# Two placements on TensorE in a fused RWKV-7 and SoLU kernel: transposes inside the solve/scores stretch of two slots, and the mean of w_out

## The chip, the core and the metric

The kernel runs on one core of one Trainium2 chip. The metric is the device time of one execution, in microseconds. Before the change it is 621.36 us, the median of 3 runs (620.54 to 622.96).

## The reference

Two blocks follow each other. The first is a linear recurrence over 768 time steps for 4 batches x 8 heads, with a state of 40 x 40 per head. The second is a feed-forward layer with 1024 hidden units over the 3072 resulting rows of 320.

```python
for t in range(S):                                   # S = 768
    y[:, :, t] = einsum('bhd,bhde->bhe', r_t, state)
    Sa = einsum('bhde,bhe->bhd', state, a_t)
    state = state * w_t[:, :, None, :] - Sa (x) b_t + v_t (x) k_t
x = y as (3072, 320)
h = x @ w_in                                         # 320 x 1024
solu = h * exp(h - max h) / (sum exp(h - max h) + 1e-9)
ln = (solu - mean(solu)) / sqrt(var(solu) + 1e-6) * g_ln
out = ln @ w_out                                     # 1024 x 320
```

## The kernel before

**Slots.** Time is cut into chunks of 64 steps, 12 per sequence, and the batches are taken in two pairs, so there are 24 pieces of work (chunk and pair), each with 128 rows: 2 batches x 64 steps. One main loop runs over slots `i` from -1 to 27. It is a software pipeline: slot `i` prepares piece `i+5` (decay, transposes, the chunk's coupling matrix `nt`), brings the inverse for piece `i+1`, does the recurrence proper of piece `i`, and does the feed-forward layer of pieces `i-2` to `i-4`. All engines run a schedule written out by hand: each engine's instructions stand in the order in which the loop body calls them, and an engine never goes past an instruction that waits. "Slot 5" below is the iteration with `i = 5`.

**The order within a slot, on TensorE.** By the names of the tiles: `pu` (the solve, `solved`, 64 passes of small products: every float32 product runs as two passes), `ps` (the scores of piece i+1, `scores`, 64 passes), `pst` (four transposes of the state, `stated`), `pa` (four transposes of the input `a` of piece i+5, `front`), a product of `h` (`hidden`), `pb` (`front_b`), `pei` (`decay_turned`), another product of `h`, `pcum` (`decay`), four products of `po` (`output`), `py` (`couple`), `pnt` (`norm`), `pl` (`answered`), the other four of `po`, `pz` (`close`), then `pyo`, `px` (`read`, `carried`, `driven`), `plnT` (`folded`), and between further products of `h` the transposes `pk`, `pv` and `pr` of the next piece (`attend_kv`, `attend_r`). Slots 0 to 3 have no feed-forward products or only some of them.

**Buffers that tie the engines together.** PSUM has three pools: `banks` (two buffers, used in turn by `pu`, `ps`, `py`, `pnt`, `pl`, `pz`, `pyo`, `px`), `bank` (two buffers, in turn for the transposes, `pcum`, `pmean` and `po`) and one buffer `h`. So `pz` takes the buffer of `pnt`, and can start when VectorE has read `pnt` (the mask that writes `nt`, L375); `pei` takes the buffer of `pa` and waits for VectorE's `aT` (L366); `pl` takes that of `py` and waits for ScalarE's `wy` (L469).

**VectorE and ScalarE.** VectorE does the masks (`psi`, `lv`, `nt`, `lu`, all L375), `aT`, the softmax part (`nmax`, `e`, statistics), the reading of `pyo` (`x` L619, `tot` L634), a block inverse in small steps (`prod` L428, `uu` L430) spread over the slots, `flip` (`tu`, L457), and the conversion of the weights. ScalarE copies transposes out of PSUM, takes exponentials and logarithms (`lw`, `ei`, `inv`), and does part of the conversion. GpSimd scales `kb` (L337) with `inv` and issues DMAs.

**The weights and their mean.** `w_in` and `w_out` arrive as 64-bit words and are converted to float32 piece by piece in slots -1 to 3 (`split`, called by `narrow`: `scale` on VectorE and ScalarE L182 to L191, then three VectorE operations L193 to L195). `w_out`, already times `g_ln`, stands in `w2` in 8 chunks of 128 rows. Its mean over the 1024 rows is summed on TensorE: the constant matrix `mean` (2^-10 everywhere) times each chunk, summed in PSUM and copied out by ScalarE (L231). It is done in three parts; a later part first brings the sum so far back with a product by the identity (L227). `centred` then subtracts the mean from `w2` in slot 4 (L236). The three calls before the change are

```python
if i == 1 + LAG:                      # slot 2, between answered (pl) and close (pz)
    mean = mean_of(0, 4)
if i == 2 + LAG:                      # slot 3, at the same place
    mean = mean_of(4, 6, mean)
...
if i == 2 + LAG:                      # slot 3, at its very end
    mean = mean_of(6, NF, mean)
```

Of the kernel before, what the change touches and what calls it, by code (L numbers as in the profile page):

```python
# [9 lines left out]
FP32 = mybir.dt.float32  # L10
# [7 lines left out]
P = 128  # L18
# [4 lines left out]
AHEAD = 5  # L23
LANDS_NEXT = {2: 6, 3: 7, 5: 8, 6: 9, 7: 10, 8: 11, 10: 12}
LAG = 1
LN_EXP = "natural_log_exp_and_others"


# [20 lines left out]
def kernel(  # L49
# [18 lines left out]
    nc = tc.nc  # L68
    B, H, S, D = r.shape
    DM = H * D  # L70
    DFF = moe_w_in.shape[1]
# [13 lines left out]
    ps2 = ctx.enter_context(tc.tile_pool(name="ps2", bufs=1, space=PSUM))  # L85
# [3 lines left out]

    nc.scalar.preload_act_table_set(LN_EXP)  # L90

# [4 lines left out]
    def c_(name):  # L96
        lo, hi = where[name]
        return cst[:, lo:hi]

    ident, tri = c_("ident"), c_("tri")  # L100
# [31 lines left out]
    w2 = const.tile([P, NF, DM], FP32, name="w2")  # L132
# [6 lines left out]
    def bank(name):  # L139
        return ps3.tile([P, 512], FP32, tag="bank", name=name)  # L140
# [56 lines left out]
    begun = []  # L197
# [23 lines left out]
            nc.scalar.mul(out=x, in_=pg[:, 0:NF], mul=2.0 ** y)  # L221


    def mean_of(lo, hi, begun=None):
        t = bank("pmean")
        if begun is not None:
            nc.tensor.matmul(t[:, 0:DM], lhsT=ident, rhs=begun, start=True, stop=False)  # L227
        for c in range(lo, hi):
            nc.tensor.matmul(t[:, 0:DM], lhsT=c_("mean"), rhs=w2[:, c, :], start=begun is None and c == lo, stop=c == hi - 1)
        mean = two.tile([P, DM], FP32, tag="osb", name="mean", bufs=1)  # L230
        nc.scalar.copy(out=mean, in_=t[:, 0:DM])  # L231
        return mean
# [35 lines left out]
    def heads(ap):  # L268
        return ap.rearrange("p (h d) -> p h d", d=D)
# [13 lines left out]
    def ok(i):  # L283
        return 0 <= i < N
# [29 lines left out]
    def logged(i):  # L314
        lw = st[i]["lw"] = two.tile([P, DM], FP32, tag="lw", name="lw", bufs=1)
        nc.scalar.activation(out=lw, in_=st[i]["raw_w"].rearrange("p h d -> p (h d)"), func=AF.Ln)

    def decay(i):
        if not ok(i):
            return  # L320
        d = st[i]
        if "lw" not in d:
            logged(i)
        t = (bank("pcum") if i > 5 else ps2.tile([P, DFF], FP32, tag="h", name="h"))[:, 0:DM]
        nc.tensor.matmul(t, lhsT=c_("cum"), rhs=d["lw"], start=True, stop=True)
        nc.scalar.activation(out=ei_t[0][:, :, 0:D], in_=heads(t), func=AF.Exp)
        inv = d["inv"] = two.tile([P, DM], FP32, tag="inv", name="inv", bufs=4)
        nc.scalar.activation(out=inv, in_=t, func=AF.Exp, scale=-1.0)
# [17 lines left out]
    def tokens(name, bufs=1):  # L346
        return two.tile([P, 2, 4, C], FP32, tag=name, name=name, bufs=bufs)
# [6 lines left out]
    def decay_turned(i):  # L354
        if not ok(i):
            return
        ex = st[i]["ex"] = ex_t[i % (AHEAD + 2)]
        nc.scalar.copy(out=ex[0:W2, :, :, 1:], in_=turned("ei", ei_t[0]))

    def front(i):  # L360
        if not ok(i):
            return
        d = st[i]
        t = turned("a", d["raw_a"])
        aT = d["aT"] = tokens("aT", AHEAD)
        nc.vector.tensor_tensor(out=aT[0:W2], in0=t, in1=d["ex"][0:W2, :, :, 0:C], op=ALU.mult)  # L366
# [92 lines left out]
    def couple(i):  # L459
        if not ok(i):  # L460
            return
        d = st[i]
        t = banks("py")
        for u in in_turn(lambda p, q, g, h: (p ^ h, p)):
            p, q, g, h = u
            j = 2 * q + g
            x = half(p ^ h)
            mm(t[half(p), h, j * Q:j * Q + Q], d["nt"][x, h, j], d["tu"][x, 4 * h + j, 0:Q])
        nc.scalar.activation(out=wy[:, :, :, 0:Q], in_=t[:, :, 0:4 * Q].rearrange("p h (j c) -> p h j c", j=4),  # L469
                             func=AF.Copy, scale=c_("neg_hi"))  # L470
# [26 lines left out]
    def stated(i):  # L497
        if not ok(i):
            return
        d = st[i]  # L500
        bp, ci = where_(i)
        if ci:
            t = bank("pst")
            for x in range(4):
                nc.tensor.transpose(out=t[0:W2, x * P:(x + 1) * P],  # L505
                                    in_=st_t[bp][:, 2 * x:2 * x + 2].rearrange("p a b -> p (a b)")[:, 0:W2], identity=ident)
            d["s"] = two.tile([P, 4, P], FP32, tag="s", name="s", bufs=1)
            nc.scalar.copy(out=d["s"][0:W2], in_=t[0:W2].rearrange("p (x t) -> p x t", x=4))
# [47 lines left out]
    def solved(i):  # L556
        if not ok(i):
            return
        d = st[i]
        t = banks("pu")  # L560
        for u in in_turn(lambda p, q, g, h: (p ^ h, q)):
            p, q, g, h = u
            at, x = (2 * h + g) * C, half(p ^ h)
            mm(t[half(q), p ^ h ^ q, at:at + C], x0[x, h, 2 * q + g], d["tu"][x, 4 * h + 2 * q + g, Q:])
        for u in in_turn(lambda p, q, g, h: (p ^ h, p)):
            p, q, g, h = u
            at, x = 256 + (2 * q + g) * D, half(p ^ h)
            mm(t[half(p), h, at:at + D], d["tu"][x, 4 * h + 2 * q + g, Q:], x0[x, h, 2 * q + g, 0:D])
        nuT = d["nuT"] = tokens("nuT")
        lu = d["lu"] = two.tile([P, H, W2], FP32, tag="lu", name="lu", bufs=1)  # L570
        nc.scalar.mul(out=nuT[0:W2], in_=t[0:W2, :, 0:256].rearrange("p b (j c) -> p b j c", j=4), mul=-1.0)
        nc.scalar.mul(out=lu.rearrange("p (j h) c -> p h j c", h=2)[:, :, :, C:],
                      in_=t[:, :, 256:256 + 4 * D].rearrange("p h (j d) -> p h j d", j=4), mul=-1.0)
# [67 lines left out]
    def left(i):  # L641

        if not ok(i):
            return
        x, xT = st[i]["x"], st[i]["xT"]
        for h in range(2):
            at = C * h
            nc.gpsimd.dma_start(out=xT[3 * D:P, h], in_=x[at:at + P - 3 * D, 2])
            for to in (Q * h, C + Q * h):
                nc.gpsimd.dma_start(out=xT[to:to + Q, 2], in_=x[at + P - 3 * D:at + D, 2])  # L650
# [82 lines left out]
    def some(n, kept=0):  # L733
        while len(steps) > kept and n:
            if next(steps[0], steps) is steps:
                steps.pop(0)
            else:
                n -= 1
# [75 lines left out]
    narrowed = {-1: (0, 1, 0), 0: (0, 1, 1), 1: (1, 0, 2), 2: (0, 1, 2), 3: (1, 0, 1)}  # L814
    for i in range(-1, N + 3 + LAG):
        j, m = i + AHEAD, i - LAG
        pieces = shares.get(i, (0, 5, 4, 4) if i % GRP else (3, 5, 4, 5))
        some_weights = narrowed.get(i, (0, 0, 0))
        if i >= 1:
            bring(i + 1)  # L820
        if i >= 0:
            load_values(i + 2)
        narrow(0, pieces[0])

        solved(i)
        if i >= 0:
            scores(i + 1)
        if i >= 0:
            load_keys(j + 3, "w")
        load_keys(j + 2, "bak")  # L830

        stated(i)
        front(j)
        hidden(m - 2, ((0, 1),))
        if i == 3 + LAG:
            centred(mean)
        narrow(some_weights[1], pieces[1])
        front_b(j)
        if ok(j + 2):
            logged(j + 2)  # L840
        decay_turned(j + 1)
        hidden(m - 2, ((1, 1),))
        flip(i + 1)
        highest(m - 2)
        scaled(j + 1)
        left(i - 1)
        decay(j + 2)
        output(m - 3, 0)

        some(pieces[2])  # L850
        couple(i + 1)
        exped(m - 2)
        norm(j)
        answered(i)
        weighed(m - 2)
        spreadof(m - 2)
        if ok(j) and j % GRP == GRP - 1:
            begin_inverse(j // GRP)
        if i == 0:
            turn_g()  # L860
        if i == 1 + LAG:
            mean = mean_of(0, 4)
        if i == 2 + LAG:
            mean = mean_of(4, 6, mean)
        output(m - 3, 1)

        close(i + 1)
        read(i, True)
        carried(i + 1)
        narrow(some_weights[2], pieces[3], ok(j) and j % GRP == GRP - 1)  # L870
        by_value(i + 2)
        if ok(m - 1):
            hidden(m - 1, ((2, 0), (2, 1)))
        fence()
        read(i, False)
        driven(i + 1)
        leave(i)
        begin_narrow(narrowed.get(i + 1, (0,))[0])
        folded(m - 2)
        hidden(m - 1, ((0, 0),))  # L880
        attend_kv(i + 2)
        hidden(m - 1, ((1, 0),))
        attend_r(i + 2)
        if i == 2 + LAG:
            mean = mean_of(6, NF, mean)
# [30 lines left out]
```

## Time and profile before

| what | value |
|---|---|
| median of 3 runs | 621.36 us (620.54 to 622.96) |
| the profiled execution | 617.47 us, its span 615.7 us |
| mean granted clock of TensorE | 0.938 of full speed |
| TensorE busy | 547.3 us (89%) |
| VectorE busy | 448.7 us (73%) |
| ScalarE busy | 265.6 us (43%) |
| GpSimd busy | 257.7 us (42%) |
| start of pu in slots 1, 2, 3, 4 | 89.59, 108.71, 136.46, 160.38 us |
| start of pu in slots 5, 6, 15, 16 | 182.09, 204.72, 399.23, 421.68 us |

All durations used below come from this one profiled execution. In the profile, "PE" is TensorE's product stream, "PEld" its weight loads, DVE is VectorE, ACT is ScalarE, POOL is GpSimd and SP the engine that only issues DMAs. L257 is the line of a helper that issues most products, so those are told apart by the tile they write. A row of a timeline merges neighbouring instructions of one kind: start, time from the first one's start to the last one's end (pipelined passes overlap), what it is, how many, and in brackets how long the engine stood still before it and what ended that. "issue" there means that nothing that the profile shows was awaited.

### The profile page before, as it was taken

What the parts mean: (1) busy time and instruction counts of PE and PEld (TensorE: products, weight loads), DVE (VectorE), ACT (ScalarE), POOL (GpSimd) and SP (SyncE); (2) the same over time, 40 slices, a digit from 0 to 9 for tenths busy, and PEclk for the clock granted to TensorE, in tenths of its full rate; (3) what the DMA queues carried; (4) which work ended last, traced back from release to release, by engine and by line L of the source; (5) the groups of instructions that cost most, each with busy time, mean ns of one, the idle gap of its engine ahead of it and who ended that gap; (6) DMA issues with size and microseconds to landing.
All of it is one profiled execution on the core that took longest, in us unless ns stands there. A gap on an engine that the chain in (4) does not pass through costs nothing.

```text
span 615.7 us, 26656 instructions
## 1 busy us (share of the span) xinstructions
PE 547.3 (89%) x11453; PEld 397.4 (65%) x11453; DVE 448.7 (73%) x1262; ACT 265.6 (43%) x548; POOL 257.7 (42%) x424
## 2 busy tenths in 40 slices
PE   4555587689899999999999999999999999999994
PEld 3334476566576777777777677777777676676652
DVE  4797978979968869868868868688698688443431
ACT  4434455454443544454454445444433343342221
POOL 3462272472452472473365355534624631322200
PEclk9666767789999999999999999999999999999998
DMA  8986895664445454564565574564532612310100
GB/s 166 156 157 132 176 176 107 139 137 84 82 105 98 94 118 94 97 118 99 94 122 97 95 127 97 111 110 82 109 56 53 122 44 44 65 35 26 28 19 21
DMA packets 213901, 59.93 MB, mean 97 GB/s; under 512 B 199120, under 2 KB 208952, under 8 KB 213784
## 3 DMA queue, kind: packets, MB, share of 16 engines
q1 hardware_dynamic: 195512, 33.78, 32.5%
q0 software_dynamic: 11568, 19.78, 13.9%
q10 hardware_dynamic: 6704, 4.67, 2.7%
q8 instruction: 90, 1.47, 1.0%
q14 instruction: 27, 0.22, 0.1%
HBM read 40.10 MB, written 13.37 MB: 87 GB/s over the span
## 4 chain that ended last, share of the span: by engine, by line
PE 71%; DVE 15%; DMA 4%; issue 3%; ACT 3%; SPq 1%; POOL 1%; ACTq 0%; DVEq 0%; POOLq 0%
PE po L723 16%; PE h L257 15%; PE pyo L257 7%; DVE prod L428 4%; DVE uu L430 4%; PE pu L257 4%; PE plnT L712 4%; PE ps L257 3%; PE px L257 3%; PE py L257 2%; PE pl L257 2%; PE pz L257 2%; PE pst L505 2%; PE pr L342 1%; PE pei L342 1%
## 5 line engine op out<-in xcount | busy, mean ns | idle before, releaser
L257 PE MATMUL h<-w_in,xT 128*128 128x512 f32 (+1 forms) x288 | 123.0, 610 | 0.0
L723 PE MATMUL po<-w,lnT 128*128 128x320 f32 x384 | 112.7, 438 | 0.5 <-ACT lnT L713 0.5
L430 DVE TENSOR_TENSOR uu<-uu,prod 128x30 f32<-128x30 f32 (+4 forms) x360 | 102.1, 284 | 12.4
L428 DVE TENSOR_TENSOR prod<-blk,uu 128x30 f32<-128x30 f32 (+4 forms) x360 | 97.6, 271 | 9.6
L723 PEld LDWEIGHTS po<-w,lnT 128*128 128x128 f32 x384 | 71.0, 190 | 32.6 <-issue 4.1
L401 POOL DMA_DIRECT2D nt_dram<-nt x20 | 18.9, 943 | 120.0 <-DVE nt L375 98.5
L375 DVE TENSOR_TENSOR psi<-ps,cst 128x512 f32<-128x512 f32 x24 | 16.6, 690 | 66.6 <-PE ps L257 66.6
L701 POOL TENSOR_TENSOR rs<-c,mhalf 128x1 f32<-128x1 f32 x24 | 13.5, 561 | 112.1 <-DVE c L700 103.2
L650 POOL DMA_DIRECT2D xT<-x x96 | 48.7, 512 | 0.0
L257 PEld LDWEIGHTS h<-w_in,xT 128*128 128x128 f32 (+1 forms) x288 | 37.4, 189 | 9.2 <-issue 8.1
L670 DVE TENSOR_REDUCE nmax<-h 128x1 f32<-128x1024 f32 x24 | 28.6, 1193 | 18.6 <-PE h L257 18.6
L412 POOL DMA_DIRECT2D blk<-nt_dram x46 | 36.6, 802 | 10.8 <-issue 6.8
L257 PE MATMUL pyo<-lv,kb 64*64 64x104 f32 x768 | 37.8, 266 | 2.2
L257 PEld LDWEIGHTS pyo<-lv,kb 64*64 64x64 f32 x768 | 23.9, 140 | 20.9 <-issue 20.8
L638 POOL TENSOR_TENSOR st<-tot,ex 104x160 f32<-104x160 f32 x44 | 21.8, 512 | 36.6 <-DVE tot L634 23.5
L257 PE MATMUL pyo<-lu,kb 64*64 64x104 f32 x768 | 36.7, 258 | 0.0
L469 ACT ACTIVATE wy<-py,cst 128x256 f32<-128x256 f32 x24 | 11.4, 473 | 56.2 <-PE py L257 56.2
L280 POOL DMA_DIRECT2D raw_r<-in_r_dram x48 | 33.9, 709 | 0.0
L727 ACT ACTIVATE osb<-po,rs 128x320 f32<-128x320 f32 x24 | 12.7, 527 | 48.5 <-PE po L723 32.9
L554 ACT COPY x<-px 128x320 f32<-128x320 f32 x24 | 10.2, 425 | 54.1 <-PE px L257 54.0
L678 ACT ACTIVATE e<-h,nmax 128x1024 f32<-128x1024 f32 x24 | 26.6, 1108 | 14.3 <-DVE nmax L670 14.3
L684 DVE TENSOR_TENSOR e<-h,e 128x1024 f32<-128x1024 f32 x24 | 29.2, 1217 | 4.6 <-ACT e L678 4.6
(128 smaller groups left out, 1162.6 us busy)
## 6 DMA issues: line engine op xcount, KB each, us to landing
blk<-nt_dram POOLq DMA_DIRECT2D x46, 128.0 KB, 4.4
nt_dram<-nt POOLq DMA_DIRECT2D x20, 256.0 KB, 3.5
raw_w<-in_w_dram SPq DMA_DIRECT2D x48, 80.0 KB
a<-in_a_dram SPq DMA_DIRECT2D x48, 80.0 KB
raw_r<-in_r_dram POOLq DMA_DIRECT2D x48, 80.0 KB, 3.1
lv<-in_v_dram SPq DMA_DIRECT2D x48, 80.0 KB
out_dram<-osb ACTq DMA_DIRECT2D x24, 160.0 KB
raw_b<-in_b_dram SPq DMA_DIRECT2D x44, 80.0 KB
```

The lines of the kernel that those rows point to most:

```text
L257: nc.tensor.matmul(o, lhsT=lhsT, rhs=rhs, start=start, stop=stop, skip_group_check=True)
L280: queue.dma_start(out=x[half(p), :, 0:D], in_=ap[2 * bp + p, :, ci * C:(ci + 1) * C, :].rearrange("h t d -> t h d"))
L412: queue.dma_start(out=nb[home:home + Q], in_=blocks[n][:, Q * e:Q * e + Q, Q * e:Q * e + Q])
L428: nc.vector.tensor_tensor(out=t, in0=nb[:, j:j + 1, j + 1:Q].to_broadcast([P, n_c, m]), in1=u[:, 0:n_c, j:j + 1].to_broadcast([P, n_c, m]) ...
L430: nc.vector.tensor_tensor(out=u[:, 0:n_c, j + 1:Q], in0=u[:, 0:n_c, j + 1:Q], in1=t, op=ALU.subtract)
L638: nc.gpsimd.tensor_tensor(out=to3(old), in0=to3(tot[0:W2]), in1=ex[:, :, 2 * q:2 * q + 2, C:].to_broadcast([W2, 2, 2, D]), op=ALU.mult)
L650: nc.gpsimd.dma_start(out=xT[to:to + Q, 2], in_=x[at + P - 3 * D:at + D, 2])
L670: nc.vector.tensor_reduce(out=nmax, in_=d["h"], axis=AX.X, op=ALU.max, negate=True)
L678: nc.scalar.activation(out=e, in_=d["h"], func=AF.Exp, bias=d["nmax"], accum_out=d["esum"])
L684: nc.vector.tensor_tensor(out=d["e"], in0=d["h"], in1=d["e"], op=ALU.mult)
L712: nc.tensor.transpose(out=t[:, j * P:(j + 1) * P], in_=d["e"][:, f * P:(f + 1) * P], identity=ident)
L723: nc.tensor.matmul(d["out"][:, 0:DM], lhsT=d["lnT"][:, f, :], rhs=w2[:, f, :], start=f == 0, stop=f == NF - 1)
```

## The change

In slots 5 and 15 the calls `stated(i)` and `front(j)`, which transpose the state of piece `i` and the input `a` of piece `i+5`, stand between `solved(i)` and `scores(i+1)` instead of after `scores(i+1)` and the loads of later pieces. On TensorE `pst` and `pa` then come before `ps`; on VectorE `aT` comes before `psi` and `lv`; on ScalarE and in the DMA queues the order stays.

The mean's first part shrinks from four chunks to three and is summed in the buffer `h`, not in a `bank`: two products stand in slot 2 between `pb` and `pei`, the third between `pei` and `pcum`, and its copy on ScalarE between `ex` and `ei`. The second part grows from two chunks to three and moves in slot 3 from behind `pl` to before `py`; its copy moves ahead of `wy` and of the exponential of `h`. The third part stays. The number of products is the same.

```diff
+THIN = (5, 15)
...
+    def mean_part(t, lo, hi, start, stop=True):
+        for c in range(lo, hi):
+            nc.tensor.matmul(t[:, 0:DM], lhsT=c_("mean"), rhs=w2[:, c, :], start=start and c == lo, stop=stop and c == hi - 1)
...
+    def mean_kept(t):
         mean = two.tile([P, DM], FP32, tag="osb", name="mean", bufs=1)
         nc.scalar.copy(out=mean, in_=t[:, 0:DM])
         return mean
...
         solved(i)
+        if i in THIN:
+            stated(i)
+            front(j)
         if i >= 0:
             scores(i + 1)
         if i >= 0:
             load_keys(j + 3, "w")
         load_keys(j + 2, "bak")
 
-        stated(i)
-        front(j)
+        if i not in THIN:
+            stated(i)
+            front(j)
         hidden(m - 2, ((0, 1),))
...
         front_b(j)
         if ok(j + 2):
             logged(j + 2)
+        if i == 1 + LAG:
+            first = ps2.tile([P, DFF], FP32, tag="h", name="mean")
+            mean_part(first, 0, 2, True, False)
         decay_turned(j + 1)
         hidden(m - 2, ((1, 1),))
         flip(i + 1)
         highest(m - 2)
         scaled(j + 1)
         left(i - 1)
+        if i == 1 + LAG:
+            mean_part(first, 2, 3, False)
+            mean = mean_kept(first)
         decay(j + 2)
         output(m - 3, 0)
 
         some(pieces[2])
+        if i == 2 + LAG:
+            mean = mean_of(3, 6, mean)
         couple(i + 1)
...
-        if i == 1 + LAG:
-            mean = mean_of(0, 4)
-        if i == 2 + LAG:
-            mean = mean_of(4, 6, mean)
         output(m - 3, 1)
```

More of the change, by code (lines that the diff above doesn't have):

```diff
@@ L221, in turn_g, with mean_of @@
             nc.scalar.mul(out=x, in_=pg[:, 0:NF], mul=2.0 ** y)
-    def mean_of(lo, hi, begun=None):
+    def mean_part(t, lo, hi, start, stop=True):
+        for c in range(lo, hi):
+            nc.tensor.matmul(t[:, 0:DM], lhsT=c_("mean"), rhs=w2[:, c, :], start=start and c == lo, stop=stop and c == hi - 1)
+    def mean_of(lo, hi, begun):
         t = bank("pmean")
[L226 to L229, printed above, removed]
+        nc.tensor.matmul(t[:, 0:DM], lhsT=ident, rhs=begun, start=True, stop=False)
+        mean_part(t, lo, hi, False)
+        return mean_kept(t)
+    def mean_kept(t):
         mean = two.tile([P, DM], FP32, tag="osb", name="mean", bufs=1)
```

## The prediction

> **What bounds the kernel now.** I read the page first: TensorE is busy for 89% of the span, and the chain that ended last is TensorE for 71% of it. The 40 slices show two regimes. Up to slice 9 (about 135 us) the clock digit jumps between 6 and 9 and VectorE is as full as TensorE; from there on TensorE is full at 9.
>
> ```profile
> PE 547.3 (89%) x11453; PEld 397.4 (65%) x11453; DVE 448.7 (73%) x1262; ACT 265.6 (43%) x548; POOL 257.7 (42%) x424
> PE   4555587689899999999999999999999999999994
> DVE  4797978979968869868868868688698688443431
> PEclk9666767789999999999999999999999999999998
> ```
>
> Both edits must therefore be read in their own stretch. For slots 5 and 15 I listed TensorE's timeline around each slot's pu (slot 5 starts at 182.09 us, slot 15 at 399.23 us; column 1 is the start, column 2 the time from first start to last end). Of all slots from 4 to 18 these two alone have a wait on TensorE:
>
> ```profile
> 182.09 0.69 PE L257 MATMUL pu<-tu,x 64*64 64x64 f32 x32
> 183.54 0.57 PE L257 MATMUL ps<-rT,vT 40*64 40x64 f32 x25
> 184.94 0.34 PE L257 MATMUL ps<-rT,vT 40*64 40x64 f32 x7 [0.83 <-issue]
> 185.21 0.64 PE L505 MATMUL pst<-cst,st 128*104 128x128 f32 x4
> ...
> 401.91 0.34 PE L257 MATMUL ps<-rT,vT 40*64 40x64 f32 x7 [0.66 <-issue]
> ```
>
> No tile is awaited ("issue"), and both stops fall after the same 25th pass of ps. The list of DMA queues between 182 and 185 us, and between 399 and 402 us, holds one packet of 16 KB on the instruction queue each time. So TensorE has run out of instructions: pu and ps are 128 passes with 128 weight loads, which it eats in some 2 us.
>
> For the mean I read the chain that ended last between 108 and 135 us (start, length, what). It runs along VectorE up to 119.5 us, then TensorE, and through the four products of the mean in slot 2:
>
> ```profile
> 121.56 0.85 PE pl L257 x32
> 122.42 4.41 PE pmean L229 x8
> 126.83 0.64 PE pz L257 x32
> 127.49 0.37 ACT tu L481
> 127.86 0.47 ACT scale L184
> ...
> 132.17 0.76 DVE x L619 x2
> ```
>
> They cost 1.1 us each, because the clock is at one half there; in slot 3 four passes take 1.08 us on the same chain. The table by stretches gives the clock (column PEclk) and TensorE's busy time in it:
>
> ```profile
> 112.88:116.30 3.42, 1.27 (x8) 0.80 (x8) 3.30 (x10) 1.03 (x3) 0.00 (x0) 1.00 0.67 124
> 116.30:119.71 3.41, 1.57 (x7) 0.64 (x10) 3.19 (x11) 2.36 (x7) 0.25 (x1) 0.50 0.58 97
> 119.71:123.12 3.41, 3.41 (x98) 3.10 (x99) 3.27 (x6) 0.88 (x3) 3.39 (x6) 0.50 0.86 191
> 123.12:126.54 3.42, 3.42 (x8) 1.94 (x6) 3.21 (x13) 0.00 (x0) 3.21 (x7) 0.50 0.53 101
> 126.54:129.95 3.41, 3.41 (x133) 2.51 (x132) 1.23 (x4) 2.82 (x7) 1.40 (x2) 1.00 0.72 128
> ```
>
> And VectorE, full from 104 us on, pays for the late pz with its longest wait of slot 2, for ScalarE's scale, which stands behind pz's copy:
>
> ```profile
> 126.68 0.18 DVE L430 TENSOR_TENSOR uu<-uu,prod 128x15 f32<-128x15 f32 x1
> 128.95 0.49 DVE L193 SCALAR_TENSOR_TENSOR bits<-bits,scale 128x320 int32<-128x320 int32 x1 [2.09 <-ACT scale L185]
> ```
>
> **Slots 5 and 15.** Nothing is added. pst (4 transposes) and pa (4) go ahead of the 64 passes of ps; from pst's start to the next product is 0.92 us (185.21 to 186.13, and 402.19 to 403.11). The order of the built program has as many instructions on TensorE as before, so the block of instructions that is short begins where it did; its last eight passes of ps (32 take 0.50, so 0.12 us) are replaced by 0.92 us of transposes. It lasts 0.80 us longer, and the new block has that much more time to land. Gap 0.83 leaves 0.03, gap 0.66 leaves nothing: 0.80 + 0.66 = 1.46. From ps's start to pst it is 2.17 and 2.00 us where slot 6 has 1.07, so the stops cost up to 1.10 and 0.93, of which 0.80 each can go: at most 1.60. The lower end is nothing, if the packet is fetched later by as much. I take 1.5, the rows of the gaps. Who waits: ps's masks on VectorE come about when they did, in a wait of 5.15 and 5.81 us for ps, and aT goes ahead of them; ScalarE copies s after lu, earlier than before. pst and pa need the banks of vT's and rT's copies, which end at 182.8 us, before pu does. The DMA issues that stood between ps and pst in the code keep their order on SP. All of it is free.
>
> The Trainium skill ("Runtime: NRT & Kernel Launch", section "Instruction fetch mechanics") says that an engine's instructions are refilled in blocks of 16 KiB, ahead of need, and that the crossing is mostly hidden. It speaks against this edit: by it 0 would be gained in these slots and 2.0 us would be the whole sum. The two gaps beside a 16 KB packet are not hidden, and I go by them.
>
> **Slot 2's mean.** Two products of w2 go ahead of pei, where TensorE stands still from 113.7 to 115.07 us for aT's multiply on VectorE; at the full clock granted there they take 1.08 us. The third goes ahead of pcum, which waits until 117.88 for lw: 0.54 us. Both holes are deep enough, and w2's chunks 0 to 2 were finished at 109.3. The copy of the mean (0.43) goes in ScalarE's queue between ex (ends 118.3) and ei (119.35), where it stood idle for 1.05. If that cover were gone, ei, and GpSimd's kb behind it, would be up to 0.43 later. The sum's bank is h's, free until slot 2's hidden product.
>
> What is late next when 4.41 us leave the path: pz needs pnt's bank, so the mask nt on VectorE, which ends at 123.5. pz then starts at about 123.6 instead of 126.75; pz, its copy and the first scale end near 126.2, before VectorE's own work at 126.86. The 2.09 us wait closes and VectorE goes on: the x of slot 2 (132.17) comes by VectorE at 126.86 + 3.22 = 130.08. TensorE must have its pyo by then: 4.24 us from pz at full clock (126.75 to 130.99), about 1.9 times that at half (pz with four pyo groups: 2.29 us in slot 1 at half, 1.20 here). With the clock back at 126.54, as now, it is 126.54 + (4.24 - 2.94/1.9) = 129.2: hidden. One stretch of 3.41 us later (129.95) it is 130.85, and 1.3 us are gained. More can come if kb on GpSimd, against which a 0.2 us step of the inverse lasted 2.17 us at 119.68, moves ahead: pcum at full clock brings ei 0.6 us forward. So 1.3 to 2.7 with the clock back in time; I take 2.0, the wait.
>
> **Slot 3's mean.** One copy product and three of w2 (8 passes, 2.2 us) go ahead of py, which waits 1.17 us for tu on VectorE; py, pnt and pl come 1.1 us later. That is hidden by nt: VectorE reaches it at 147.04, pnt then ends at 146.2, and pz stays at 147.8, with 6 passes fewer in front of it. ScalarE's Exp of h comes 1.2 us later, ending near 147.5; its reader is VectorE's e at 148.24. Cost 0, up to 0.4 if that 0.7 of room is used up. The last two products stay. Slots 3 and 4 are VectorE's and later ones TensorE's without a wait, so a gain of slot 2 is carried to the end.
>
> The sum: 2.0 + 1.5 = 3.5 us. The profiled execution took 617.47 us (span 615.7), so 614.0; the median is 621.36 us, 3.9 above it, for which no row accounts, and I carry the difference over: 617.9 us.
>
> **Rivals.** (a) The fetch moves with the crossing and starves TensorE elsewhere: only the 2.0 of slot 2, 619.4 us. For it: the count of instructions is the same, so the crossings stay where they are in the stream. Against: all other 16 KB packets pass without a stop. (b) Slot 2's gain is taken up by VectorE, which has nt, narrowing and the inverse in one queue and was the bound up to 119.5 us: 1.5 only, 619.9 us. Against: the 2.09 us is an idle wait of just that engine. (c) The clock. The half state ended at 126.54 after two stretches that were busy to the full, with the mean in them. Without it they are busy for about 2.6 and 2.9 of 3.41 us. After 99.23 a stretch of 3.05 did not bring the clock back and the next of 3.31 did. If it stays at half beyond 133.4 us, TensorE comes last (its pk and pv then reach ScalarE after its scales) and each further stretch costs 3.41 - 3.41/1.9 = 1.6 us: three more, to about 143.6, give 4.8 - 1.5, so 624.7 us. For it: removing dense work at the point where the clock rises. Against: the added products lift the stretch from 112.88 from 1.27 to about 2.9 us busy, and stretches of 2.56 and more kept the clock. (d) More: kb moved ahead and a shorter half state, 2.7 + 1.6 and up to a stretch's 1.6 besides: 617.1 to 615.5 us.
>
> On (c), the Trainium skill ("TensorE: Matmul & The Clock Gate", Part 1) has the clock fall after an idle window of about 3.4 us; here it fell after one with 1.27 us of work, so the measured row is stricter. By the page's rule the filled holes of slot 2 would not matter to the clock, and the sum stays 3.5.
>
> **How the numbers follow.** Forecast 0.48 (alone 616.8 to 619.0); (a) 0.13; (b) 0.13; (c) 0.11, of which about half is mild; (d) 0.15. The range leaves out the far ends of (c) and (d): 615.3 to 621.8. About 0.5% (3.1 us) is what a measurement can tell from no change. The forecast stands only 0.4 beyond that, so two thirds of it counts as faster, with (d) and a little noise 0.52; 0.40 within; 0.08 slower.
>
> **What would show it.** Right: no issue gap, or one under 0.1, in ps of slots 5 and 15, with ps's first to last start some 1.0 us as in slot 6; mean's first products between pb and pei in slot 2; pz within 0.2 us of nt's end; VectorE's 2.09 us wait gone; slot 3's start some 2 us earlier (pu of slot 3 at 134.4 instead of 136.46) and slot 5's too. Wrong: the gap at another pass or slot, half a clock beyond 130 us, or pz waiting for something later than nt.

## The result and the profile after

The changed kernel takes 618.94 us (median of 22 runs, 614.10 to 622.93) beside 620.94 us of the kernel before (22 runs in the same series): the ratio of the runs is 0.9959, 95% interval 0.9944 to 0.9975 (the two medians alone give 0.9968), so 1.6 to 3.5 us are gained. Two later series of the same kernel gave 0.9944 (0.9921 to 0.9966) and 0.9967 (0.9945 to 0.9990). The forecast of -3.5 us lies at the edge of the first interval.

The profiled execution of the changed kernel took 618.02 us, which is more than the 617.47 us of the kernel before. The two must not be subtracted: up to slot 1 the programs are the same, and there the second one is already 3.3 us later (slot 1's x on VectorE starts at 109.29 us before and at 112.60 us after). The clock rows of the two pages differ there, in slices 3 and 6 (6 and 7 before, 5 and 5 now; lines of the changed kernel stand 8 lower: helper L257 is L265, the masks L375 are L383, x is L627):

```profile
PE 552.0 (90%) x11453; PEld 401.9 (65%) x11453; DVE 449.0 (73%) x1262; ACT 265.8 (43%) x548; POOL 258.0 (42%) x424
PEclk9665765789999999999999999999999999999998
```

Slot 2 on TensorE's timeline (start, length, what, and the wait before it). The first products of the mean fill the hole ahead of pei, the third stands ahead of pcum, and pz now waits for nt and for nothing else:

```profile
117.67 1.24 PE L229 MATMUL mean<-w,cst 128*128 128x320 f32 x4
118.75 0.60 PE L350 MATMUL pei<-cst,ei 128*104 128x128 f32 x4
119.19 0.70 PE L229 MATMUL mean<-w,cst 128*128 128x320 f32 x2
126.88 0.67 PE L265 MATMUL pz<-uh,wy 64*64 64x32 f32 x32 [2.05 <-DVE nt L383]
```

VectorE's wait of 2.09 us for ScalarE's scale is gone; from slot 1's x to slot 2's x it takes 20.48 us instead of 22.88. Slot 5 on the same timeline:

```profile
184.08 0.65 PE L513 MATMUL pst<-cst,st 128*104 128x128 f32 x4
184.56 0.60 PE L350 MATMUL pa<-cst,a 128*104 128x128 f32 x4
185.60 0.45 PE L265 MATMUL ps<-rT,vT 40*64 40x64 f32 x17
186.22 0.46 PE L265 MATMUL ps<-rT,vT 40*64 40x64 f32 x15 [0.17 <-issue]
```

The stop sits after the 17th pass of ps instead of the 25th, as eight passes of transposes now stand ahead of it among TensorE's instructions, and 0.17 us of it is left; in slot 15 none. Yet slot 5 (from pu's start to the next pu's) goes only from 22.63 to 22.34 us and slot 15 from 22.45 to 21.87. That is 0.87 us, not 1.5, and the first question for the experiments.

### The profile page after: what moved, and what is told of

Its sections match the earlier page's. It is cut to its first block, busy times and chain, and to the rows that moved or that the text cites. A ratio compares the mean times of both kernels' runs of the same rounds, so it can differ in the third digit from the quotient of the medians.

```text
span 616.2 us, 26656 instructions
## 1 busy us (share of the span) xinstructions
PE 552.0 (90%) x11453; PEld 401.9 (65%) x11453; DVE 449.0 (73%) x1262; ACT 265.8 (43%) x548; POOL 258.0 (42%) x424
## 4 chain that ended last, share of the span: by engine, by line
PE 74%; DVE 17%; ACT 3%; issue 3%; DMA 1%; ACTq 1%; DVEq 0%; SPq 0%
PE po L731 16%; PE h L265 16%; PE pyo L265 8%; DVE uu L438 5%; DVE prod L436 5%; PE pu L265 4%; PE plnT L720 4%; PE ps L265 4%; PE px L265 3%; PE py L265 2%; PE pl L265 2%; PE pz L265 2%; PE pr L350 2%; PE pst L513 2%; PE pcum L333 1%
## 5 line engine op out<-in xcount | busy, mean ns | idle before, releaser
L265 PE MATMUL h<-w_in,xT 128*128 128x512 f32 (+1 forms) x288 | 123.7, 614 | 0.0
L436 DVE TENSOR_TENSOR prod<-blk,uu 128x30 f32<-128x30 f32 (+4 forms) x360 | 99.2, 276 | 9.6
L383 DVE TENSOR_TENSOR psi<-ps,cst 128x512 f32<-128x512 f32 x24 | 16.6, 690 | 59.5 <-PE ps L265 59.5
L265 PEld LDWEIGHTS h<-w_in,xT 128*128 128x128 f32 (+1 forms) x288 | 37.6, 190 | 9.4 <-issue 8.1
L265 PE MATMUL pyo<-lv,kb 64*64 64x104 f32 x768 | 38.3, 269 | 2.2
L265 PEld LDWEIGHTS pyo<-lv,kb 64*64 64x64 f32 x768 | 24.1, 142 | 21.2 <-issue 21.1
L265 PE MATMUL pyo<-lu,kb 64*64 64x104 f32 x768 | 37.4, 262 | 0.1
```

Source lines behind the costliest of these rows:

```text
L265: nc.tensor.matmul(o, lhsT=lhsT, rhs=rhs, start=start, stop=stop, skip_group_check=True)
L436: nc.vector.tensor_tensor(out=t, in0=nb[:, j:j + 1, j + 1:Q].to_broadcast([P, n_c, m]), in1=u[:, 0:n_c, j:j + 1].to_broadcast([P, n_c, m]) ...
```

## The experiments

There were twelve runs, some of them of the same kernel again. Two questions have two theories each: whether a change between small and full-size products has a price (A) or the order is free (B), and whether slot 2's gain depends on where the clock is at half (C) or is the 2.4 us of the first two profiles always (D). Because the profiled executions differ by up to 4 us before slot 2, where all programs are the same, the profiles are compared by two lengths that leave this out: on VectorE's timeline from the start of slot 1's x to that of slot 2's x, and on TensorE's from pu to pu. The column "clock back" is the end of the half-clock stretch that began in slot 2, counted from slot 1's x.

| profile | mean | order in 5, 15 | slot 1's x | clock back | x to x | pz to x | slot 5 | slot 15 |
|---|---|---|---|---|---|---|---|---|
| before | old | old | 109.29 | 17.25 | 22.88 | 5.42 | 22.63 | 22.45 |
| e9_before_again | old | old | 112.67 | 15.73 | 22.14 | 5.43 | 22.47 | 22.30 |
| e1_thin_alone | old | new | 112.52 | 15.95 | 22.24 | 5.42 | 22.06 | 22.16 |
| e10_thin_again | old | new | 110.76 | 15.84 | 22.18 | 5.42 | 22.21 | 21.85 |
| e3_order_in_steady_slots | old | old | 112.53 | 14.88 | 21.71 | 5.42 | 22.91 | 23.27 |
| after | new | new | 112.60 | 18.78 | 20.48 | 6.20 | 22.34 | 21.87 |
| e5_changed_again | new | new | 112.87 | 20.19 | 21.50 | 7.21 | 22.03 | 21.86 |
| e12_both_again | new | new | 110.65 | 24.06 | 22.30 | 8.01 | 22.03 | 21.89 |
| e2_mean_alone | new | old | 112.29 | 18.86 | 20.50 | 6.21 | 23.29 | 22.84 |
| e11_mean_again | new | old | 110.98 | 20.15 | 21.48 | 7.19 | 22.91 | 22.99 |
| e4_h_ahead | new | other | 111.23 | 22.03 | 22.27 | 7.99 | | |
| e8_longer_block | new | other | 111.96 | 20.42 | 21.57 | 7.29 | | |
| e6_filler | new, two products more | new | 113.13 | no fall | 20.37 | 6.07 | 22.03 | 22.38 |
| e7_mean_left_out | last part only | new | 112.76 | 19.37 | 21.09 | 6.80 | 22.48 | 22.70 |

**One part alone, twice.**

```diff
 # e1_thin_alone, e10_thin_again: the mean as before
-        if i == 1 + LAG:
-            first = ps2.tile([P, DFF], FP32, tag="h", name="mean")
-            mean_part(first, 0, 2, True, False)
...
+        if i == 1 + LAG:
+            first = bank("pmean")
+            mean_part(first, 0, 4, True)
...
 # e2_mean_alone, e11_mean_again: the order as before
-THIN = (5, 15)
+THIN = ()
```

> Only the reordering of slots 5 and 15; the mean is summed as before. Theory A (each change between full-size transposes and the small products of pu and ps has a price, about 0.33 us for the two more of them in a slot, and only the rest of the stop is gained): slots 5 and 15 take 22.3 and 21.9 us instead of 22.63 and 22.45, together about 0.9 us less, ratio 0.9985 or so. Theory B (the order itself is free, as predicted, and what is missing in the changed kernel is chance in when the packet of instructions comes): 1.5 us less, ratio 0.9976, both slots near 21.6. Slots 2 and 3 as before under both: 9.7 us from psi's start to nt's in slot 2, and about 9.3 from nt to x.

> Only the mean moved; slots 5 and 15 in the old order. Theory A: nearly all of the gain is here, 2.4 us (nt to x in slot 2 about 6.9 us instead of 9.32, VectorE's wait of 2.09 us gone), ratio 0.996, and slots 5 and 15 take 22.6 and 22.4 us again. Theory B: 2.0 us or less, ratio 0.997, the rest being the reordering's.

Measured: e1_thin_alone 0.9987 (0.9964 to 1.0010), e2_mean_alone 1.0006 (0.9982 to 1.0029). Neither theory had the mean without a gain in time while its slot 2 was as short as after (20.50 us). Both profiles held something else, a stop in slot 9, which took 25.02 and 25.03 us instead of 21.53. So they were repeated with the kernel before and with both parts in one series:

> The kernel before, unchanged, beside the next three, for a second profile of it and for what the comparison makes of two equal kernels. Theory E (the first profile was early: its slot 1 had its x at 109.3 us, all eight other profiles at 111.2 to 113.1, with the same program up to there): x of slot 1 at 111 to 113, slot 1's x to slot 2's x 21.7 to 22.9, slots 5 and 15 at 22.5 to 23.3 with an issue gap of 0.7 to 1.5 in ps, ratio 1.000 within 0.002.

> The reordering alone once more. Theory A with the stops as measured since (slots 5 and 15: mean 22.9 in the old order, 22.1 in the new): 1.6 us less, ratio 0.9974. If the first result (0.9987) was the whole of it, 0.8 us.

> The mean alone once more. Theory C (mean of slot 1's x to slot 2's x: 22.3 old, 21.3 new): 1.0 us less, ratio 0.998. Theory D: 2.4 us, 0.996. If the first result (1.0006) was the whole of it: no gain.

> Both parts once more on this chip: the sum of the two, 2.6 us, ratio 0.9958, whichever of them it comes from; slot 1's x to slot 2's x between 20.4 and 22.3.

Measured: 1.0005 (0.9983 to 1.0027) for the equal kernel, 0.9980 (0.9960 to 1.0001) for the order, 0.9988 (0.9968 to 1.0009) for the mean, 0.9967 (0.9945 to 0.9990) for both. In this series the product of the parts, 0.9968, is what both give. By these times the order is worth about 1.2 us and the mean about 0.7, each within 1.3 us; together with the first series it is 1.0 and 0.2. So the times alone don't show that the mean gains by itself; that rests on the profiles below.

**The price of the order, nine times over.** The reordering in slots 6 to 14, with the old mean:

```diff
-THIN = (5, 15)
+THIN = tuple(range(6, 15))
```

> The kernel before with the reordering in slots 6 to 14 instead, where TensorE never stopped in ps, so that only its price is left, nine times over. Theory A: each of these slots takes about 0.33 us more (21.85 instead of 21.53), 3.0 us in all, ratio 1.005, and the rows ps to h or pa to ps show it. Theory B: no change, 21.53 us a slot, ratio 1.000.

Measured: 1.0082 (1.0041 to 1.0123). Its slots 8, 10, 13 and 14 take 21.85 or 21.86 us where they took 21.52 or 21.53 before: 0.33 us a slot, as theory A had it. Slot 6 rises by 0.34, but slots 7, 11 and 12, which were longer before, only by 0.24, 0.23 and 0.01, so that the nine prices come to about 2.5 us and not to 3.0. TensorE's timeline of slot 10 shows where, first before, then with the new order:

```profile
291.70 0.63 PE L257 MATMUL pu<-x,tu 64*64 64x40 f32 x32
292.14 0.67 PE L257 MATMUL ps<-aT,kT 40*64 40x64 f32 x32
...
294.13 1.02 PE L257 MATMUL h<-w_in,xT 128*128 128x512 f32 x2
294.99 0.60 PE L342 MATMUL pb<-cst,kb 128*104 128x128 f32 x4
```

```profile
296.33 0.63 PE L265 MATMUL pu<-x,tu 64*64 64x40 f32 x32
296.88 0.65 PE L513 MATMUL pst<-cst,st 128*104 128x128 f32 x4
297.37 0.60 PE L350 MATMUL pa<-cst,a 128*104 128x128 f32 x4
297.90 0.70 PE L265 MATMUL ps<-aT,kT 40*64 40x64 f32 x32
298.99 1.12 PE L265 MATMUL h<-w_in,xT 128*128 128x512 f32 x2
299.95 0.60 PE L350 MATMUL pb<-cst,kb 128*104 128x128 f32 x4
```

From the second half of pu to pb it is 3.29 us before (291.70 to 294.99) and 3.62 with the new order: 0.11 is lost from pu to pst (0.55 where pu to ps takes 0.44), 0.09 from pa to ps (0.53 for 0.44), 0.10 in h, the first full-size product behind ps (0.96 for 0.86). All stand at a change between small products and full-size ones, of which the new order has two more. The time rose by 5 us (from five executions), twice these prices. In the profiled executions the spans of e3 and e9, 622.7 and 617.6 us, differ by as much: by 3.3 us in slots 6 to 14, of which 1.0 is slot 9, where e3 stopped for 0.49; by 1.4 in slots 5 and 15, where e3's stops were 1.10 and 1.48 us and e9's 0.66 and 0.51; and by 0.4 in slot 21. So in that one execution the stops make up most of the rest.

**Other fillings of the block.**

```diff
 # e4_h_ahead (slots 5, 15) and e8_longer_block (slots 5, 9, 15, 19)
+        if i in THIN:
+            hidden(m - 2, ((0, 1),))
         solved(i)
-        if i in THIN:            # in e4: pst and pa behind ps again
-            stated(i)
-            front(j)
...
-        hidden(m - 2, ((0, 1),))
+        if i not in THIN:
+            hidden(m - 2, ((0, 1),))
```

> The changed kernel, but in slots 5 and 15 the first product of h (two passes, 0.86 us) goes ahead of pu in place of the transposes between pu and ps, which stand after ps again. The block of instructions lasts as much longer, but small and full-size products change no more often than before. Theory A: about 0.33 us per slot better than the changed kernel, slots 5 and 15 at 21.6 to 21.9, 0.6 us in all, ratio to before 0.995. Theory B: as the changed kernel, 0.996, with slots 5 and 15 the same within 0.1.

> The changed kernel, with the first product of h ahead of pu and also pst and pa between pu and ps, in slots 5, 9, 15 and 19. The block that runs out then lasts 1.6 us longer instead of 0.8. If the stop is only the packet coming late (0.7 to 1.5 us in slots 5 and 15, up to 1.7 in slot 9), there is no issue gap left in any of the four and slots 5, 9 and 15 take 21.9 us; 0.5 us less than the changed kernel in slots 5 and 15 together, about 1.5 less where slot 9 stopped; slot 19 pays 0.3. Ratio to before 0.994 to 0.996. If the stop goes with the crossing, gaps of 0.4 or more remain.

Measured: e4 1.0007 (0.9983 to 1.0032), e8 0.9963 (0.9942 to 0.9984) beside 0.9944 of the changed kernel in e8's series. In e4 a product of h crosses the line between two slots, so pairs count: slots 4 and 5 take 44.61 us and 14 and 15 44.43, while the changed order took 43.75 to 44.06 and 43.39 (after, e5). Theory A's forecast for it fell: gaps of 0.38 and 0.39 us stay in ps, and pb waits another 0.33 for the copy of s, which h had hidden. e8 has no issue gap in any of the four slots, here in slot 5:

```profile
185.98 0.60 PE L350 MATMUL pa<-cst,a 128*104 128x128 f32 x4
186.51 0.69 PE L265 MATMUL ps<-aT,kT 40*64 40x64 f32 x32
187.02 0.65 PE L265 MATMUL ps<-rT,vT 40*64 40x64 f32 x32
187.60 0.65 PE L350 MATMUL pb<-cst,kb 128*104 128x128 f32 x4
```

That is what a packet coming late by at most 1.6 us demands, but only slots 5 and 15 test it: in slots 9 and 19 the packet came early in this execution, as in those that do not stop there (last section). And its pairs of slots take 43.68 (4, 5), 43.48 (8, 9) and 43.46 (14, 15), so work of 1.6 us ahead of the stop buys nothing over the 0.8 us of the changed kernel, and slot 9 pays 0.4 where it does not stop. Neither is a better kernel.

**The clock in slot 2.**

```diff
 # e6_filler, after answered(i), ahead of close
+        if i == 1 + LAG:
+            fill = ps2.tile([P, DFF], FP32, tag="h", name="fill")
+            mean_part(fill, 0, 2, True)
 # e7_mean_left_out: only mean_part(first, 6, NF, True) at the end of slot 3 remains
```

> The changed kernel once more, beside the others of this call. Theory C (slot 2's gain depends on where the half-clock stretch falls: VectorE's way from slot 1's x to slot 2's x took 22.9, 22.2 and 21.7 us with the old mean, 20.5, 20.5 and 22.3 with the new): 20.5 or 22.3 again according to whether the half state covers pyo, and a ratio of 0.996 to 0.998. Theory D (the gain of slot 2 is the 2.4 us of the first two profiles, always): 20.5, ratio 0.996 or less.

> The changed kernel with two products of w2 more in slot 2, between pl and pz where TensorE waits 2.05 us for nt; their sum is read by nobody. Theory C: the stretch before pz is no longer idle enough for the clock to fall, pz to x takes 5.4 us instead of 6.2 or 8.0, and slot 1's x to slot 2's x 19.7 to 20.0. If the clock is at half when they run, they take 2.2 us, more than is left of the wait, and pz comes up to 1 us later. Theory D: the clock plays no part, so 20.5 as before, or more by what the products delay pz.

> All of the mean's products and copies in slot 2 and in slot 3 ahead of py are left out (the mean subtracted is then only that of the last two chunks). Theory D (the moved products are hidden and the rest is VectorE's): slot 1's x to slot 2's x 20.5 and slot 3 23.5 from x to x, as in the changed kernel. Theory C: pz comes no earlier, 0.7 us after nt, but the stretches before it are emptier, so the clock falls to half earlier and pz to x takes 8 us rather than 6.2: 22 to 22.5.

Measured: e5 0.9944 (0.9921 to 0.9966), e6 0.9961 (0.9943 to 0.9979), e7 1.0023 (0.9994 to 1.0051). The tables by stretches (length, busy time of PE, PEld, DVE, ACT and POOL, then the granted clock) of the changed kernel's two profiles after and e12, and of e6:

```profile
124.55:127.96 3.41, 1.36 (x84) 1.19 (x80) 3.27 (x10) 0.35 (x2) 3.41 (x7) 1.00 0.88 198
127.96:131.38 3.42, 3.42 (x82) 2.84 (x75) 3.15 (x13) 3.35 (x8) 1.67 (x4) 0.50 0.39 91
```

```profile
117.65:121.06 3.41, 0.94 (x10) 0.44 (x14) 3.18 (x11) 3.09 (x8) 0.25 (x1) 1.00 0.58 97
121.06:124.47 3.41, 2.63 (x96) 2.44 (x94) 3.27 (x6) 0.47 (x1) 3.39 (x6) 0.50 0.99 209
124.47:127.89 3.42, 2.96 (x92) 2.96 (x96) 3.21 (x13) 1.78 (x4) 3.21 (x7) 0.50 0.39 82
127.89:131.30 3.41, 3.32 (x52) 1.67 (x48) 3.00 (x8) 2.43 (x6) 1.39 (x2) 0.50 0.70 125
```

```profile
125.24:128.65 3.41, 2.63 (x86) 1.86 (x78) 3.27 (x10) 0.48 (x2) 3.41 (x8) 1.00 0.78 181
128.65:132.07 3.42, 3.33 (x129) 2.46 (x120) 3.15 (x14) 3.35 (x8) 1.53 (x3) 1.00 0.38 89
```

After, one stretch at half follows the stretch with 1.36 us of work; in e12 the stretches lie otherwise, the clock falls at 121.06 after 0.94 us of work, and it stays at half for four stretches, up to 134.7 us, three of which are busy for 2.6 to 3.3 us. In e12 TensorE comes last, which VectorE's timeline of e12 says in one row:

```profile
132.95 0.75 DVE L627 TENSOR_TENSOR x<-pyo,ex 104x256 f32<-104x256 f32 x2 [1.96 <-PE pyo L265]
```

With the filler the stretch ahead of pz holds 2.63 us and the clock stays at full; x to x is then 20.37, the shortest of all. That stretch lies alike in the two, 12.1 us behind slot 1's x in e6 and 12.0 in after (1.36 us of work, and a fall), so the filler and not the place of the stretch is the likely cause, from one execution each. pz to x is 6.07 and not 5.4 as theory C had it: from nt to x VectorE needs 6.81 of its own. In time the filler gained nothing over the changed kernel, so it is no better version. e7 shows pz no earlier without any of the moved products (0.73 us after nt's start, as with them), so these cost nothing; and the clock was at half from 121.9 to 132.1 us and again from 149.2 to 156.0. Its x to x of 21.09 lies between the theories. Its time is no measure of the mean, as its stream is 32 instructions shorter and stops elsewhere (0.45 and 0.89 us in slots 5 and 15, 1.26 in slot 19). Theory D is refuted by e5, e12, e4 and e11; theory C's two values were too few, as 21.5 stands between them. The table shows what sets the value: sorted by when the clock is back, x to x rises without an exception, with the old mean (14.88 to 17.25, 21.71 to 22.88 us) and with the moved or shortened one (18.78 to 24.06, 20.48 to 22.30 us).

## Why the prediction was right, and where its terms were off

**Slots 5 and 15: the sum right, by two errors that cancel.** Forecast 1.5 us. Over the profiles with the old order slot 5 takes 22.84 us and slot 15 22.77 (five each, e3 among them), with the new order 22.13 and 21.93 (five each): 0.71 + 0.84 = 1.55, by their spread within some 0.8 (with e6, whose order is new too, it is 1.49). But "All of it is free" was wrong: the order costs 0.33 us a slot. And the stops are larger than in the first profile: its gaps of 0.83 and 0.66 are near the low end of 0.51 to 1.48 in old-order profiles, as e2's slot 5 shows:

```profile
186.19 0.34 PE L265 MATMUL ps<-rT,vT 40*64 40x64 f32 x7 [1.48 <-issue]
```

So more was there to be covered than the 0.83 and 0.66, and a part went to the price. That the one offset the other is luck. In the trace the 16 KB packet starts between 0.39 us before and 0.86 us after pu in these two slots, over the profiles with the old or the new order in them; the later it starts, the longer is the gap as a rule. This isn't the whole of it: a start of 0.06 us after pu left 0.66 us in one case (e9) and 1.21 in another (e11), and from the packet's start to the product behind the stop it was 2.4 to 3.2 us over the old-order stops.

That TensorE runs out of instructions there is shown by a count. The 14 profiles hold 29 stops of TensorE of 0.15 us or more that end on "issue". In every one the number of TensorE's instructions ahead of it in the trace (products, weight loads and the sequencer's own) is 193 or 194 beyond a multiple of 256, whatever product stands there. In slots 5 and 15 it is the same number in both orders, as the prediction had it; and in e7, whose stream is 32 instructions shorter, the stop of slot 5 falls at that number again, now behind ps, in a product of h:

```profile
188.58 0.59 PE L265 MATMUL h<-w_in,xT 128*128 128x512 f32 x1 [0.45 <-issue]
```

That work ahead of this place buys time is shown by the changed kernel and by e8, where no gap is left. The Trainium skill ("Runtime: NRT & Kernel Launch", section "Instruction fetch mechanics"), by which the crossing is mostly hidden, is borne out for nearly all of some 90 packets, and not here.

**Slot 2: the mechanism right, the size not.** Forecast 2.0 us (1.3 to 2.7). The wait closed, pz came at nt, TensorE's holes held the products, as said. The step that failed is the term itself, VectorE's 2.09 us wait of one profile. In e1, e10, e9 and e3 that wait is 1.45, 1.39, 1.33 and 0.91 us, in the order in which the clock is back (15.95, 15.84, 15.73 and 14.88 us behind slot 1's x; 17.25 in the first profile): it depends on how much of the old mean ran at half clock. The smallest, in e3:

```profile
131.01 0.49 DVE L196 SCALAR_TENSOR_TENSOR bits<-bits,scale 128x320 int32<-128x320 int32 x1 [0.91 <-ACT scale L188]
```

And the 129.2 us at which pyo was to be hidden held only "with the clock back in time". Over five profiles with the old mean x to x is 22.23 us, over seven with the new one 21.44: 0.8 us less, by the spread within some 0.8; a single profile with the new mean lies between nothing (e12) and 1.8 us (after) below 22.23.

**Rival (c) came in part.** The clock at half over pyo is what took the difference. The forecast's factor of 1.9 was good: 4.24 x 1.9 = 8.06 us from pz to x, measured 7.99 and 8.01 (e4, e12). It was given 0.11 and priced as a loss; as the old mean pays for the half clock too, it cancels the gain and no more. Its lines on the clock's return hold when counted from slot 1's x. The clock back at 129.95 us, 20.66 behind that x, was to leave 1.3 us of the 2.0: e11's, back 20.15 behind, has an x to x 1.4 below the 22.88 of the first profile. Back at 133.4 us, 24.1 behind, TensorE was to come last: e12's, back 24.06 behind, has no gain left against the 22.23. So these prices held; later than 20.66 us behind slot 1's x the clock came back in two of the seven profiles with the new mean (e4, e12).

**Slot 3: right.** Slot 2's x to slot 3's x is 23.51 us before and after, so the move is neither gain nor cost; where it is longer (23.8), this is so with the old mean (e3) and with the new one (e5, e11). **Rival (b)** is refuted by after and e6, **rival (a)** by e8 and by the two slots themselves.

**The 3.9 us between the first profile and the median**, for which no row accounted, lie for some 3 us ahead of slot 2: slot 1's x comes at 109.29 us there and at 110.65 to 113.13 in every other profile. Up to that x the clock was at half for 61.5 us there and for 64.8 to 83.5 in the others, which may be part of the cause. It isn't all: e10 and e5, with 71.7 us each, have their x at 110.76 and 112.87.

The measured parts, 1.55 + 0.8 = 2.35 us, agree with the ratios (0.9959, 0.9944, 0.9967: 2.0 to 3.5 us). That the time fell into the forecast's range says little by itself, as 615.3 to 621.8 us also holds the 620.94 of the kernel before; the rows above say more.

## What to carry to other kernels

One profile shows one phase of the clock and one arrival of the instruction packets: a wait that hangs on either is a range, and its size should be read from several executions before it is put in a sum. Where TensorE stops on "issue" at a fixed count of instructions, longer work put ahead of that count buys up to its own length, less what the change between product shapes costs. Where matmuls are taken out of a stretch on the path, look at what is left in each stretch of 3.41 us, since the clock of the work behind it hangs on that among other things.

## What the runs showed of the hardware that was not expected

Slot 9 stops in some executions and not in others. In e10_thin_again's timeline of TensorE:

```profile
272.97 0.84 PE L265 MATMUL ps<-rT,vT 40*64 40x64 f32 x32 [1.70 <-issue]
273.74 1.09 PE L513 MATMUL pst<-cst,st 128*104 128x128 f32 x4
```

The same stop of 1.70 us is in e1 and e2, one of 0.49 in e3, and none in the ten other profiles. e2 and e11 are one kernel, with it and without it, so the program alone does not decide; that all three profiles with a new order and the old mean have it may be chance, which was not tried. In these four profiles the packet that is awaited, the 36th of the 90 on that queue, starts 0.1 to 0.5 us after slot 9's pu; in the ten others the same packet starts 2.9 to 4.5 us before it. The 1.70 us stop also drops the clock to half for one stretch, which is why the slot loses 3.5 us in all.

Slot 19 does the same, and the changed kernel's first profile has it:

```profile
487.83 0.58 PE L265 MATMUL ps<-rT,vT 40*64 40x64 f32 x24 [0.89 <-issue]
```

This stop is also in e10 and e11, and one of 1.26 us in e7; there the 74th packet starts 0.2 to 0.6 us after slot 19's pu, in the ten others 3.2 to 4.3 us before it. It costs little, as TensorE's wait for tu on VectorE behind it is 0.3 us instead of 0.7 to 1.5. What decides when a packet is asked for stays open; the spread of 6 us and more within a series may partly be this.

The Trainium skill ("TensorE: Matmul & The Clock Gate", Part 1) lets the clock rise after one busy window of about 3.4 us. Here, in e12, three stretches busy for 2.63, 2.96 and 3.32 us did not bring it back, and before, the stretch from 119.71 to 123.12 us, busy throughout, was followed by another at half; they hold small products for the most part, which may matter, but no run tested that. Nor does the busy time alone say when it falls: it fell after stretches with 2.21 and 2.29 us of work (e4, at 123.02 and 150.33 us) and held after one with 1.76 (e1, at 118.24).
